# Small factors in five pieces, a second accumulator for the last attention outputs, and a reordered POOL tail in a one-core adaLN block

## The chip, the cores and the metric

The kernel runs on one NeuronCore of one Trainium2 chip. The metric is device time in microseconds of one execution. The kernel before has a median of 2770.61 us over 3 runs (2769.95 to 2776.88). In this text PE is the matrix engine, DVE the vector engine, ACT the scalar engine, POOL the GpSimd engine and SP the engine that issues the DMAs.

## The reference

One transformer block with a conditioning vector: attention over the last 512 cached keys, then a gated MLP. Everything is float32.

```python
mod = (silu(c) @ w_mod).reshape(1, 6, 1, 576)      # sa, ca, ga, sb, cb, gb
h = layernorm(x) * (1 + ca) + sa                    # x: 2048 x 576
q = h @ wq                                          # 32 heads of 128
p = softmax(q @ k[:, -512:].T * 128 ** -0.5)        # 16 key/value heads, each shared by 2 heads
x = x + ga * ((p @ v[:, -512:]) @ wo)               # wo: 4096 x 576
h = layernorm(x) * (1 + cb) + sb
x = x + gb * ((silu(h @ w1) * (h @ w3)) @ w2)       # w1, w3: 576 x 4608, w2: 4608 x 576
```

## The kernel before, in words

**Number format.** Each float32 operand of a matrix product is scaled by a power of two and split into a high and a low float16 half; a product is the sum of three float16 matmuls (high by high, high by low, low by high). The scales come from largest absolute values. For the MLP they stand in one small tile called `table`, and `act_factors` (L1180) works out from them the factors by which activations and outputs are scaled back: ten or eleven tiny DVE instructions on 4 to 28 columns, L1186 to L1199.

**Attention.** The 2048 rows are four blocks of 512. The work is a list of 128 slots, each one head on one block. A slot has four steps, t = 0 to 3, one per 128 rows. In step t, PE writes scores into a PSUM bank `pss` (L483); DVE takes the negative row maximum (L487, L488); ACT does the exponential into `p` (L500). Three of the four tiles are split on ACT and POOL and transposed by DMA; the fourth is transposed on PE into a bank `pt` (L523) and split by ACT and by DVE (`turn_low`, L552) into `ptw`. PE then forms the values `po` (L562); DVE scales them (L571), and ACT and POOL split the result into `o`.

**Output products.** Two slots make a pair. For each of the four row tiles of a pair, `back` (L428) multiplies both slots' `o` by the output weights: two pieces of six matmuls into one two-bank accumulator `E` (its tile is called `pe`, L433), and then DVE adds it to the residual `acc` (L590). Before, all pieces use the one accumulator `E`. The pieces of a pair are spread over the steps of later slots; those of the last two pairs lie in slot index n = 128 and n + 1, after the last scores.

**MLP.** The first dimension of the two input weights is cut in two and the products follow a seven-product scheme for 2 x 2 blocks: per group g of 128 hidden columns and per pair of row blocks there are seven products, in the order p1, p2, p6, p7, p5, p3, p4, each of seven matmuls (L847, into `py` or `px`). There are 36 groups for each of two pairs of row blocks. In between, DVE and ACT make the gated activations (L1017 to L1035), which are split again (L93, L94). The output products of the group pair before, called units below, are placed after single products: six matmuls (L932) into one of two accumulators that take turns, `pe` (`E`) and `pf`, and a DVE addition (L926). A counter `lane[0]` picks the accumulator, and `spare()` (L1118) returns the current one. `lane[1]` stays empty until the attention is over, and then `spare()` returns `E`. The second accumulator `pf` takes the two PSUM banks in which attention had its transposes `pt`; the pool of those (`turning`) is closed and the new one opened at L1605.

**Order.** Nothing is reordered by a scheduler: each engine runs its instructions in program order. Tasks hung on a step by `at`, `step_at` and `late_at` run in program order after that step's own work. `act_factors` runs twice: for column pairs 0 to 13 in slot 125 after step 1 (L1493), and for pairs 14 to 17 in MLP group 27 after product p2 (L1357). The first MLP group begins in slot 127, inside the attention.

**The tail.** The output products of the last group are made plainly, without the seven-product scheme: after its p6, p7, p5 and p3 there is one unit `plain(0, 0, t)` each (L934), after p4 come four units `plain(0, 1, t)`, and behind the last product four `plain(1, 1, t)` and four `plain(1, 0, t)`. Each is six matmuls into `pe` or `pf` and a DVE addition (L943). `finish` (L886) and `finish_first` (L893) add kept sums to `acc` on POOL; `finish_first(1, t)` is issued before behind `plain(0, 0, t)`. The split of the last activation, called p2 here, is made on ACT and POOL after the last product (L93, L94, tile `akv`); the p4 activation before it is split on ACT and DVE (tile `aal`).

Of the kernel before, what the change touches and what calls it, by code (L numbers as in the profile page):

```python
# [9 lines left out]
F32 = mybir.dt.float32  # L10
# [17 lines left out]
ST = SB // P  # L28
# [4 lines left out]
NF = F // P  # L33
HALF = D // 2
# [4 lines left out]
G = NF // 2  # L39
# [9 lines left out]
def tile_block(  # L49
# [14 lines left out]
    nc = tc.nc  # L64
# [16 lines left out]
    E = psum.tile([P, 2, 512], F32, tag="E", name="pe", bufs=1)  # L81
    turning = ExitStack()
# [342 lines left out]
                for k in (0, 1):  # L425
                    nc.tensor.matmul(ps, w[:, k, DC, :], hT[:, 2 * DC, :], start=False, stop=False)

    def back(o, w, t, first, last):  # L428

        rows = slice(t * P, (t + 1) * P)  # L430
        for n, (x, y) in enumerate(((0, 0), (0, 1), (1, 0))):
            for h in range(2):
                nc.tensor.matmul(  # L433
                    E[:, h, :HALF],
                    o[:, x, rows],
                    w[:, y, h * HALF : (h + 1) * HALF],
                    start=first and n == 0,
                    stop=last and n == 2,
                )
# [11 lines left out]
    n = len(slots)  # L451
# [97 lines left out]
    def turn_low(i, t):  # L549
        cols = slice(t * P, (t + 1) * P)  # L550
        pt = state[i]["pt"]
        nc.vector.tensor_sub(pt[:, 1, :, cols], state[i]["t"], pt[:, 0, :, cols])  # L552
# [30 lines left out]

    def attend_out(pair, t, j, total):
        u, _, b = slots[2 * pair]
        back(state[2 * pair + j]["o"], wos[u][:, j], t, j == 0, j == 1)
        if j == 1:
            run(*total)
            a = half_split(acc[b][:, t, :])
            nc.vector.scalar_tensor_tensor(  # L590
                a, E[:, :, :HALF], factors[:, uses[u][0], 2:3], a, op0=ALU.mult, op1=ALU.add
            )


# [131 lines left out]
    FEW = 8  # L726
# [163 lines left out]
    def finish_first(pair, t, eng):  # L890

        a = half_split(acc[2 * pair][:, t, :])
        eng.tensor_add(a, a, msums[pair][0][t])  # L893
# [40 lines left out]
    def plain(j, i, t):  # L934

        d = 2 * G - 1
        lane[0] += 1
        ps = lane[1][lane[0] % 2]
        w = osets[d, 3 if j else 4]
        multiply(ps, [(halves[d, ("p1", "p7", "p2", "p4")[2 * j + i]], w[:, h], t) for h in range(2)])  # L940
        a = half_split(acc[2 + i][:, t, :])
        factor = out_down[:, chunks(d) : chunks(d) + 1]
        nc.vector.scalar_tensor_tensor(a, ps[:, :, :HALF], factor, a, op0=ALU.mult, op1=ALU.add)  # L943
        if j == 0 and i == 0:
            finish_first(1, t, nc.gpsimd)
        elif j:
            store_out(2 + i, t)

    def act_steps(g, k):
# [98 lines left out]
    def at(i, t, task, *args):  # L1048

        tasks.setdefault((i, t), []).append((task, args))  # L1050
# [126 lines left out]
        a = works["o", p][:, 2 * part : 2 * part + 2]  # L1177
        nc.scalar.activation(a, a, AF.Copy, scale=works["n", p])

    def act_factors(lo, hi):  # L1180

        top, h_down = mlp_small[:, 2:3], mlp_small[:, 5:6]
        both = stats.rearrange("p (g j) k -> p g j k", j=2)[:, lo:hi]
        downs, pairs = both[:, :, :, 0], both[:, :, :, 1]
        a = acts_down[:, lo:hi]
        nc.vector.tensor_max(a, pairs[:, :, 0], pairs[:, :, 1])  # L1186
        nc.vector.tensor_scalar(a, a, top, 2.5 * D * 2.0**-13.5, op0=ALU.mult, op1=ALU.mult)
        nc.vector.tensor_scalar(a, a, top, 2.0**-60, op0=ALU.mult, op1=ALU.max)
        d = in_down[:, 2 * lo : 2 * hi]
        nc.vector.tensor_scalar(d, d, h_down, None, op0=ALU.mult)  # L1190
        for j in range(2):
            nc.vector.reciprocal(pairs[:, :, j], a)
            nc.vector.tensor_mul(pairs[:, :, j], pairs[:, :, j], downs[:, :, j])
        if hi == G:
            hi += 1
            nc.vector.tensor_copy(acts_down[:, G : G + 1], acts_down[:, G - 1 : G])
        d = out_down[:, lo:hi]
        nc.vector.tensor_scalar(d, d, mlp_gate_down, None, op0=ALU.mult)
        nc.vector.tensor_mul(d, d, acts_down[:, lo:hi])  # L1199

    def find(into, u, k, *key):
        find_peak(uses[u][0], k, into[(u, *key) if key else u])
# [131 lines left out]
    def late_at(step, task, *args):  # L1334
        at(("m", step // len(ORDER)), step % len(ORDER), task, *args)

    turns = len(items[ITEMS:]) // 4
    for late in range(turns):
# [15 lines left out]
            plan += [(step, make, number + k, maker, w, k), (step + STORE, store_now, number + k)]  # L1354
        for step, task, *args in plan:
            late_at(total + step, task, *args)
    late_at(2 * len(ORDER) * turns + len(ORDER) + 1, act_factors, (NF - FEW) // 2, G)  # L1357
    for k, (i, t) in enumerate(((n - 4, 0), (n - 4, 2), (n - 3, 0), (n - 2, 0))):
        at(i, t, load_wset, 0, k)

# [129 lines left out]
    at(109, 2, make_cols, "gain", "b", 4, 1.0, "T")  # L1490
    at(109, 3, lambda: spread_peaks("b", mlp_small))
    at(110, 1, lambda: scale_cols("b", t_bank(), mlp_small, 2.0**-8))
    at(n - 3, 1, act_factors, 0, (NF - FEW) // 2)  # L1493
    for b in (2, 3):
        for t in range(ST):
            at(b + 1, t, load_x, b, (t,))
# [61 lines left out]
    for i in range(n + 2):  # L1558
        run(i, -1)
        for t in range(ST):  # L1560
# [10 lines left out]
                normalize(i - 2)  # L1571
            if 1 <= i <= n and t == 2:
                turn_low(i - 1, ST - 1)
            if t == 3 and i + 1 < n:
                query_low(i + 1)
            if i < n:
# [37 lines left out]

def packed(inputs):
# [63 lines left out]
```

## Time and profile before

The profiled execution took 2773.59 us, with a span of 2771.7 us from first to last instruction.

| | |
|---|---|
| runs: median (lowest, highest) | 2770.61 us (2769.95, 2776.88) |
| profiled execution, its span | 2773.59 us, 2771.7 us |
| mean granted clock of PE | 0.992 |
| PE busy | 2692.8 us, 97% of the span |
| DVE, ACT, POOL busy | 72%, 58%, 68% |
| attention with its outputs | up to about 1632 us |
| MLP alone | from there to the end |

Every time below is in microseconds from the start of the span. A row of the timeline is start, duration, engine, line, operation, tiles (written <- read), shape and count; in square brackets stands how long the engine had been idle before it and what ended that wait. Matmuls are pipelined, so a row of six matmuls shows 0.90 us where the next may start 0.74 us after it. A row of the view by windows is the stretch, its length, the busy time and count of PE, its weight loads, DVE, ACT and POOL, then the granted PE clock, the share of the DMA engines and GB/s.

### The profile page before, as it was taken

What the parts mean: (1) busy time and instruction counts of PE and PEld (TensorE: products, weight loads), DVE (VectorE), ACT (ScalarE), POOL (GpSimd) and SP (SyncE); (2) the same over time, 40 slices, a digit from 0 to 9 for tenths busy, and PEclk for the clock granted to TensorE, in tenths of its full rate; (3) what the DMA queues carried; (4) which work ended last, traced back from release to release, by engine and by line L of the source; (5) the groups of instructions that cost most, each with busy time, mean ns of one, the idle gap of its engine ahead of it and who ended that gap; (6) DMA issues with size and microseconds to landing.
All of it is one profiled execution on the core that took longest, in us unless ns stands there. A gap on an engine that the chain in (4) does not pass through costs nothing.

```text
span 2771.7 us, 44752 instructions
## 1 busy us (share of the span) xinstructions
PE 2692.8 (97%) x15406; PEld 1515.9 (55%) x15406; DVE 1999.8 (72%) x3555; ACT 1617.5 (58%) x3013; POOL 1881.9 (68%) x1748
## 2 busy tenths in 40 slices
PE   6899999999999999999999999999999999999998
PEld 3455555555555555555555555555555555555554
DVE  7877787877788787877876667777776666666666
ACT  5777778777777778787677634544443333333332
POOL 5578788888788877777669537688873465333435
PEclk8999999999999999999999999999999999999999
DMA  5778888788787788979889935656643434333332
GB/s 184 174 174 195 196 177 192 169 184 192 160 185 167 191 186 201 206 182 213 184 190 223 239 112 171 200 170 199 213 135 108 160 121 128 104 103 111 104 110 78
DMA packets 593460, 463.84 MB, mean 167 GB/s; under 512 B 442704, under 2 KB 472528, under 8 KB 592208
## 3 DMA queue, kind: packets, MB, share of 16 engines
q1 hardware_dynamic: 592944, 460.69, 64.9%
q8 instruction: 121, 1.98, 0.3%
q14 instruction: 107, 0.88, 0.1%
q10 hardware_dynamic: 288, 0.30, 0.0%
HBM read 264.19 MB, written 95.99 MB: 130 GB/s over the span
## 4 chain that ended last, share of the span: by engine, by line
PE 52%; DVE 2%; issue 1%; ACT 1%; POOL 1%; DMA 0%; SPq 0%; DVEq 0%; ACTq 0%; POOLq 0%
PE py L847 15%; PE px L847 11%; PE pe L932 7%; PE pf L932 7%; PE pe L433 3%; PE po L562 3%; PE pss L483 3%; PE pq L410 2%; PE pt L523 0%; PE pq L414 0%; DVE table L487 0%; DVE acc L590 0%; DVE on L571 0%; DMA r<-row 0%; ACT p L500 0%
## 5 line engine op out<-in xcount | busy, mean ns | idle before, releaser
L537 POOL TENSOR_TENSOR hp<-p,hp 128x512 f16<-128x512 f32 x384 | 450.2, 1175 | 271.0 <-ACT hp L532 147.9
L500 ACT ACTIVATE p<-pss,table,factors 128x512 f32<-128x512 f32 x512 | 396.9, 775 | 360.9 <-DVE table L488 186.6
L847 PEld LDWEIGHTS <-wset 128*128 128x128 f16 x3528 | 344.6, 98 | 337.9 <-issue 5.3
L487 DVE TENSOR_REDUCE table<-pss 128x1 f32<-128x512 f32 x512 | 350.3, 684 | 209.9 <-PE pss L483 205.9
L847 PE MATMUL py<-hset,wset 128*128 128x512 f16 x2016 | 483.6, 380 | 0.0
L433 PE MATMUL pe<-o 128*128 128x288 f16 x3072 | 459.6, 286 | 15.8 <-DVE acc L590 15.3
L483 PE MATMUL pss<-k,qT 128*128 128x512 f16 x1536 | 420.1, 381 | 13.7 <-ACT p L500 10.3
L433 PEld LDWEIGHTS <-o 128*128 128x128 f16 x3072 | 300.7, 98 | 189.6 <-issue 22.4
L562 PE MATMUL po<-ptw,v 128*128 128x512 f16 x1536 | 359.3, 382 | 10.4 <-DVE ptw L552 5.5
L847 PE MATMUL px<-hset,wset 128*128 128x512 f16 x1512 | 361.6, 379 | 1.6 <-ACT p L500 1.6
L410 PE MATMUL pq<-hT,wq 128*128 128x512 f16 x1092 | 283.2, 382 | 1.0 <-POOL hT L254 0.7
L94 POOL TENSOR_TENSOR akv<-u,akv 128x512 f16<-128x512 f32 x141 | 165.0, 1180 | 174.3 <-ACT akv L93 166.5
L532 ACT CAST hp<-p 128x512 f16<-128x512 f32 x384 | 237.3, 618 | 13.2 <-POOL hT L256 0.6
L562 PEld LDWEIGHTS <-v 128*128 128x128 f16 x1536 | 148.2, 98 | 175.4 <-issue 19.4
L932 PEld LDWEIGHTS <-akv 128*128 128x128 f16 x1728 | 169.6, 98 | 93.8 <-issue 4.8
L483 PEld LDWEIGHTS <-qT 128*128 128x128 f16 x1536 | 147.9, 98 | 129.0 <-issue 15.6
L590 DVE SCALAR_TENSOR_TENSOR acc<-pe,factors,acc 128x576 f32<-128x576 f32 x256 | 207.7, 811 | 10.4 <-PE pe L433 10.4
L582 POOL TENSOR_TENSOR o<-on,o 128x512 f16<-128x512 f32 x128 | 150.4, 1175 | 55.6 <-ACT o L581 52.7
L410 PEld LDWEIGHTS <-wq 128*128 128x128 f16 x1092 | 107.5, 98 | 129.7 <-issue 4.6
L926 DVE SCALAR_TENSOR_TENSOR acc<-pf,table,acc 128x576 f32<-128x576 f32 x140 | 113.4, 810 | 80.3 <-PE pf L932 80.3
L1027 ACT COPY u<-py 128x512 f32<-128x512 f32 x72 | 42.2, 586 | 202.1 <-PE py L847 200.2
L1020 ACT ACTIVATE s<-s,table 128x512 f32<-128x512 f32 x72 | 52.0, 722 | 173.9 <-DVE s L1019 173.9
(244 smaller groups left out, 4791.2 us busy)
## 6 DMA issues: line engine op xcount, KB each, us to landing
wset<-wd SPq DMA_DIRECT2D x213, 320.0 KB, 3.2
r<-row SPq DMA_DIRECT2D x128, 256.0 KB, 3.9
oset<-od SPq DMA_DIRECT2D x106, 288.0 KB, 3.2
wraw<-in_w SPq DMA_DIRECT2D x36, 768.0 KB, 5.7
wd<-wmade SPq DMA_DIRECT2D x75, 320.0 KB, 3.3
wset<-wd SPq DMA_DIRECT2D x71, 160.0 KB, 2.3
w2raw<-in_w SPq DMA_DIRECT2D x19, 576.0 KB, 5.3
wd<-ring SPq DMA_DIRECT2D x33, 320.0 KB, 2.8
```

The costliest lines, as they stand in the source:

```text
L94: eng.tensor_sub(halves[:, 1], src, halves[:, 0])
L410: nc.tensor.matmul(ps, w[:, k // 2, m, :], hT[:, DC + m if k == 1 else m, :], start=s == 0, stop=False)
L433: nc.tensor.matmul(E[:, h, :HALF], o[:, x, rows], w[:, y, h * HALF : (h + 1) * HALF], start=first and n == 0, stop=last and n == 2,)
L483: nc.tensor.matmul(pss, q[:, x, rows], k[:, y, :], start=n == 0, stop=n == 2)
L487: nc.vector.tensor_reduce(nm[:, 0:1], pss, axis=AX.X, op=ALU.max, negate=True)
L500: nc.scalar.activation(p, pss, AF.Exp, bias=nm[:, 1:2], scale=factor, accum_out=st["l"][:, t : t + 1])
L532: nc.scalar.copy(hp[:, 0, :], state[i]["p", t])
L537: nc.gpsimd.tensor_sub(hp[:, 1, :], state[i].pop(("p", t)), hp[:, 0, :])
L562: nc.tensor.matmul(po, v[:, x, c, :], pt[:, y, c, :], start=c == 0 and n == 0, stop=c == KC - 1 and n == 2)
L590: nc.vector.scalar_tensor_tensor(a, E[:, :, :HALF], factors[:, uses[u][0], 2:3], a, op0=ALU.mult, op1=ALU.add)
L847: nc.tensor.matmul(ps, w[:, a, :], h[:, b, :], start=start and n == 0, stop=stop and n == 6, skip_group_check=True)
L932: nc.tensor.matmul(ps[:, h, :HALF], a[:, rows], w[:, b, :], start=m == 0, stop=m == 2)
```

## The change

There are three edits.

First, `act_factors` takes a piece number from 0 to 4 and issues only that part of its instructions. Each of its two calls becomes five calls in five successive steps: the early one in slot 124 after steps 2 and 3 and slot 125 after steps 0, 1 and 2, the late one in group 27 after p2, p6, p7, p5 and p3.

Second, `back` is handed its accumulator. `attend_out` advances `lane[0]` at the first piece of a row tile and asks `spare()`, and the pool of transposes is closed, and `pf` opened, in slot index 128 step 2 behind the last `turn_low`. The last two pairs' eight row tiles so use `pf` and `pe` in turn; all earlier tiles still use `pe`.

Third, `finish_first(1, t)` is issued behind `plain(1, 1, t)` instead of behind `plain(0, 0, t)`.

```diff
-    def back(o, w, t, first, last):
+    def back(ps, o, w, t, first, last):
...
-                    E[:, h, :HALF],
+                    ps[:, h, :HALF],
...
     def attend_out(pair, t, j, total):
         u, _, b = slots[2 * pair]
-        back(state[2 * pair + j]["o"], wos[u][:, j], t, j == 0, j == 1)
+        lane[0] += j == 0
+        ps = spare()
+        back(ps, state[2 * pair + j]["o"], wos[u][:, j], t, j == 0, j == 1)
...
-                a, E[:, :, :HALF], factors[:, uses[u][0], 2:3], a, op0=ALU.mult, op1=ALU.add
+                a, ps[:, :, :HALF], factors[:, uses[u][0], 2:3], a, op0=ALU.mult, op1=ALU.add
...
-        if j == 0 and i == 0:
-            finish_first(1, t, nc.gpsimd)
-        elif j:
+        if j:
             store_out(2 + i, t)
...
-    def act_factors(lo, hi):
+    def act_factors(lo, hi, piece):
...
-        nc.vector.tensor_max(a, pairs[:, :, 0], pairs[:, :, 1])
-        nc.vector.tensor_scalar(a, a, top, 2.5 * D * 2.0**-13.5, op0=ALU.mult, op1=ALU.mult)
-        nc.vector.tensor_scalar(a, a, top, 2.0**-60, op0=ALU.mult, op1=ALU.max)
-        d = in_down[:, 2 * lo : 2 * hi]
-        nc.vector.tensor_scalar(d, d, h_down, None, op0=ALU.mult)
-        for j in range(2):
+        if piece == 0:
+            nc.vector.tensor_max(a, pairs[:, :, 0], pairs[:, :, 1])
+            nc.vector.tensor_scalar(a, a, top, 2.5 * D * 2.0**-13.5, op0=ALU.mult, op1=ALU.mult)
+        elif piece == 1:
+            nc.vector.tensor_scalar(a, a, top, 2.0**-60, op0=ALU.mult, op1=ALU.max)
+            d = in_down[:, 2 * lo : 2 * hi]
+            nc.vector.tensor_scalar(d, d, h_down, None, op0=ALU.mult)
+        elif piece < 4:
+            j = piece - 2
             nc.vector.reciprocal(pairs[:, :, j], a)
             nc.vector.tensor_mul(pairs[:, :, j], pairs[:, :, j], downs[:, :, j])
...
-    late_at(2 * len(ORDER) * turns + len(ORDER) + 1, act_factors, (NF - FEW) // 2, G)
+    for piece in range(5):
+        late_at(2 * len(ORDER) * turns + len(ORDER) + 1 + piece, act_factors, (NF - FEW) // 2, G, piece)
...
-    at(n - 3, 1, act_factors, 0, (NF - FEW) // 2)
+    for piece in range(5):
+        step_at(ST * (n - 4) + 2 + piece, act_factors, 0, (NF - FEW) // 2, piece)
...
                 turn_low(i - 1, ST - 1)
+                if i == n:
+                    turning.close()
+                    after = ctx.enter_context(tc.tile_pool(name="after", bufs=1, space=PSUM))
+                    lane[1] = (E, after.tile([P, 2, 512], F32, tag="T2", name="pf"))
...
-    turning.close()
-    after = ctx.enter_context(tc.tile_pool(name="after", bufs=1, space=PSUM))
-    lane[1] = (E, after.tile([P, 2, 512], F32, tag="T2", name="pf"))
     for _ in stream:
         pass
     for i in (1, 0):
         for t in range(ST):
             plain(1, i, t)
+            if i:
+                finish_first(1, t, nc.gpsimd)
```

What remains in the last piece (4) is the copy of one column and the two instructions on `out_down`.

How rows move on DVE in MLP group 27, before. `table` holds the factors, `acc_89`, `acc_90`, `acc_91` and `acc_92` are the residual of row blocks 0 to 3, `sums` are kept sums, and L926 is the addition behind each unit:

```order
L1186 TENSOR_TENSOR table<-table 128x4
L1187 TENSOR_SCALAR table<-table 128x4
L1188 TENSOR_SCALAR table<-table 128x4
L1190 TENSOR_SCALAR table<-table 128x8
L1192 RECIPROCAL table<-table 128x4
L1193 TENSOR_TENSOR table<-table 128x4
L1192 RECIPROCAL table<-table 128x4
L1193 TENSOR_TENSOR table<-table 128x4
L1196 COPY table<-table 128x1
L1198 TENSOR_SCALAR table<-table 128x5
L1199 TENSOR_TENSOR table<-table 128x5
L926 SCALAR_TENSOR_TENSOR sums_18991<-pe,table,sums_18991 128x576
```

All eleven rows stand in one block ahead of the next addition. In the changed kernel (its lines are two to three higher: L928 is the addition, L1187 the first factor), on the same engine and place, from piece 1 on and down to the last piece:

```order
L1190 TENSOR_SCALAR table<-table 128x4
L1192 TENSOR_SCALAR table<-table 128x8
L928 SCALAR_TENSOR_TENSOR acc_89<-pf,table,acc_89 128x576
L1195 RECIPROCAL table<-table 128x4
L1196 TENSOR_TENSOR table<-table 128x4
L1028 TENSOR_TENSOR u_23232<-px,u_23232 128x512
L928 SCALAR_TENSOR_TENSOR acc_89<-pe,table,acc_89 128x576
```

```order
L1032 SCALAR_TENSOR_TENSOR u_23232<-u_23232,table,s_23261 128x512
L94 TENSOR_TENSOR aal<-u_23232,aal 128x512
L1200 COPY table<-table 128x1
L1202 TENSOR_SCALAR table<-table 128x5
L1203 TENSOR_TENSOR table<-table 128x5
L1034 TENSOR_TENSOR u_23184<-px,u_23184 128x512
L1035 SCALAR_TENSOR_TENSOR u_23184<-u_23184,table,s_23133 128x512
L928 SCALAR_TENSOR_TENSOR acc_89<-pe,table,acc_89 128x576
```

The factors now stand two or three at a time between the additions, and the last three of them stand ahead of the two steps that make the p4 activation and of the addition behind p4.

On DVE at the last two pairs' output products, in the changed kernel:

```order
L592 SCALAR_TENSOR_TENSOR acc_92<-pe,factors,acc_92 128x576
L552 TENSOR_TENSOR ptw<-pt,ptw 128x4x128
L1034 TENSOR_TENSOR u_18654<-px,u_18654 128x512
L1035 SCALAR_TENSOR_TENSOR u_18654<-u_18654,table,s_18581 128x512
L592 SCALAR_TENSOR_TENSOR acc_91<-pf,factors,acc_91 128x576
L592 SCALAR_TENSOR_TENSOR acc_91<-pe,factors,acc_91 128x576
L592 SCALAR_TENSOR_TENSOR acc_91<-pf,factors,acc_91 128x576
L592 SCALAR_TENSOR_TENSOR acc_91<-pe,factors,acc_91 128x576
```

The order of this engine is the one before; only the accumulator that is read has become `pf` for every other row tile, the first of them behind L552.

On POOL at the very end of the program, before and then in the changed kernel:

```order
L886 TENSOR_TENSOR sums<-sums 128x288
L893 TENSOR_TENSOR acc_91<-acc_91,sums 128x576 x4
L94 TENSOR_TENSOR akv<-u_29481,akv 128x512
L1674 UNCONDITIONAL_BRANCH
```

```order
L888 TENSOR_TENSOR sums<-sums 128x288
L94 TENSOR_TENSOR akv<-u_29481,akv 128x512
L895 TENSOR_TENSOR acc_91<-acc_91,sums 128x576 x4
L1683 UNCONDITIONAL_BRANCH
```

The four additions of 576 columns have changed places with the split of the last activation. The order of ACT and of SP, with all its DMAs, is the same in both kernels.

More of the change, by code (lines that the diff above doesn't have):

```diff
@@ L1185, in act_factors @@
         a = acts_down[:, lo:hi]
-        nc.vector.tensor_max(a, pairs[:, :, 0], pairs[:, :, 1])
-        nc.vector.tensor_scalar(a, a, top, 2.5 * D * 2.0**-13.5, op0=ALU.mult, op1=ALU.mult)
-        nc.vector.tensor_scalar(a, a, top, 2.0**-60, op0=ALU.mult, op1=ALU.max)
-        d = in_down[:, 2 * lo : 2 * hi]
-        nc.vector.tensor_scalar(d, d, h_down, None, op0=ALU.mult)
-        for j in range(2):
+        if piece == 0:
[7 more added lines that the diff above has]
+            j = piece - 2
             nc.vector.reciprocal(pairs[:, :, j], a)
             nc.vector.tensor_mul(pairs[:, :, j], pairs[:, :, j], downs[:, :, j])
[L1194 to L1199, printed above, removed]
+        else:
+            if hi == G:
+                hi += 1
+                nc.vector.tensor_copy(acts_down[:, G : G + 1], acts_down[:, G - 1 : G])
+            d = out_down[:, lo:hi]
+            nc.vector.tensor_scalar(d, d, mlp_gate_down, None, op0=ALU.mult)
+            nc.vector.tensor_mul(d, d, acts_down[:, lo:hi])
     def find(into, u, k, *key):
```

## The prediction

> **What bounds the kernel now.** I read the windows first, to see where PE, the engine that sets the end, is not busy, and then its waits over the whole run, the longest first.
>
> ```profile
> 1544.00:1597.00 53.00, 47.52 (x266) 26.13 (x265) 33.01 (x64) 33.25 (x65) 29.20 (x26) 1.00 1.01 252
> 1597.00:1633.00 36.00, 31.11 (x189) 18.25 (x187) 15.17 (x20) 8.62 (x14) 9.61 (x8) 1.00 0.30 90
> 2030.00:2060.00 30.00, 26.32 (x136) 14.01 (x134) 23.87 (x36) 11.00 (x19) 17.85 (x16) 0.89 0.34 106
> 2060.00:2740.00 680.00, 678.40 (x3927) 383.77 (x3925) 416.68 (x543) 215.74 (x369) 302.93 (x258) 1.00 0.38 117
> 2740.00:2771.70 31.70, 23.10 (x134) 13.49 (x132) 19.79 (x23) 3.76 (x6) 16.12 (x16) 0.93 0.20 75
> ...
> PE pe L433 <- DVE acc L590: 15.3, 15, 2.4
> PE po L562 <- DVE ptw L552: 5.5, 8, 2.9
> ```
>
> PE is busy 678.4 of 680 us in the long stretch of the MLP, so whatever delays it there is paid in full. The change touches the four short stretches, in which PE idles 5.5, 4.9, 3.7 and 8.6 us and, in the last two, also loses clock (0.89 and 0.93). In each, DVE is what PE waits for. A microsecond taken from these waits is a microsecond off the end, unless another releaser is right behind.
>
> **Early factors (slots 124 and 125).** Rows of the timeline:
>
> ```profile
> 1548.61 2.75 PE L562 MATMUL po<-ptw,v 128*128 128x512 f16 x12
> ...
> 1557.52 1.22 POOL L537 TENSOR_TENSOR hp<-p,hp 128x512 f16<-128x512 f32 x1 [0.62 <-ACT hp L532]
> 1557.75 1.02 DVE L1187 TENSOR_SCALAR table<-table 128x14 f32<-128x14 f32 x1
> 1560.19 0.59 PE L562 MATMUL po<-ptw,v 128*128 128x512 f16 x2
> 1562.02 0.18 DVE L1199 TENSOR_TENSOR table<-table 128x14 f32<-128x14 f32 x1
> 1562.96 0.68 DVE L552 TENSOR_TENSOR ptw<-pt,ptw 128x512 f16<-128x512 f32 x1
> 1563.70 2.32 PE L562 MATMUL po<-ptw,v 128*128 128x512 f16 x10 [2.91 <-DVE ptw L552]
> ```
>
> The ten instructions hold DVE from 1557.5 to 1562.1, 4.6 us for 14 columns: L1187 ends with the POOL instruction beside it, at 1558.74, so it is waiting, not computing. L552 is queued behind them, and PE's third value matmul, due two spacings of 0.22 after 1560.19, starts at 1563.70: **3.07 us lost**. The clock stays at 1.00. Cut in five, the pieces last about 1.2, 2.4, 0.4, 0.4 and 0.5 to 1.8 us. By the windows row DVE is busy 33.0 of 53 us, 28.4 without the block, so 46% is free: about 1.3 us in each step (a slot of four steps lasts 11.6, from 1548.61 to 1560.19, the same place of the next slot). Piece 1 overdraws a step by 1.1 us, and behind it stand row maxima, whose exponential PE needs two steps later. I take the whole 3.0. The lower bound is 0: PE would come 3 us earlier to the MLP's first operands, which are loaded late.
>
> ```profile
> 1582.79 0.42 SPq L699 DMA_DIRECT2D hset<-hd  x1
> 1593.75 1.67 PE L847 MATMUL py<-hset,wset 128*128 128x512 f16 x7
> hset<-hd SPq DMA_DIRECT2D x6, 1280.0 KB, 7.9
> ```
>
> Issued at 1582.79 and 7.9 us in flight, that set lands near 1590.7, 3.06 us ahead of its product. If nothing of the load moved forward, the gain would just fit; the DMA engines' share of 1.01 in this stretch says the fit may fail.
>
> **Second accumulator (last two pairs).**
>
> ```profile
> 1600.65 0.68 DVE L552 TENSOR_TENSOR ptw<-pt,ptw 128x512 f16<-128x512 f32 x1
> 1600.79 1.63 PE L433 MATMUL pe<-o 128*128 128x288 f16 x12 [0.43 <-DVE acc L590]
> 1603.50 1.63 PE L433 MATMUL pe<-o 128*128 128x288 f16 x12 [1.08 <-DVE acc L590]
> ...
> PE pe L433 <- DVE acc L590: 4.9, 5, 1.6
> ```
>
> Five of the eight row tiles start late, 4.9 us in all, since each must wait until DVE has emptied the one accumulator. Four of these waits (4.9 less 0.43) vanish, and with each 0.16 us of refilling the matmul pipeline (a six-matmul row lasts 0.90, but the next step follows after 0.73 where nothing waits; rows below): 4.46 + 0.65 = 5.1. The first tile pays: it now writes `pf`, whose banks held transposes until L552 ends at 1601.33, so it starts near 1601.4 instead of 1600.79, **0.6 later**. Queued behind it are only the tiles that gain. DVE is 42% busy here (15.2 of 36), so the additions keep up. Sum **4.5 us**; bounds 2.0, if ACT's exponential-to-silu steps of the MLP group become the next wait at two of the four places, and 4.6.
>
> **Late factors (group 27).** First the undisturbed step lengths from the chain of waits, then the timeline there, then one later group of the same kind.
>
> ```profile
> 2744.32 0.73 PE pe L932 x6
> 2745.05 1.51 PE py L847 x7
> ...
> 2036.93 1.13 DVE L1187 TENSOR_SCALAR table<-table 128x4 f32<-128x4 f32 x1
> 2038.95 1.67 PE L847 MATMUL py<-hset,wset 128*128 128x512 f16 x7
> 2042.45 1.07 DVE L1199 TENSOR_TENSOR table<-table 128x5 f32<-128x5 f32 x1
> 2044.30 1.60 PE L932 MATMUL pe<-oset,akv 128*128 128x288 f16 x6 [3.68 <-DVE sums L926]
> 2047.14 3.19 PE L847 MATMUL py<-hset,wset 128*128 128x512 f16 x7
> 2050.12 1.78 PE L847 MATMUL px<-hset,wset 128*128 128x512 f16 x7
> ...
> 2083.20 0.90 PE L932 MATMUL pe<-oset,akv 128*128 128x288 f16 x6
> 2085.95 1.04 DVE L1035 SCALAR_TENSOR_TENSOR u<-u,table,s 128x512 f32<-128x512 f32 x1
> ```
>
> The block holds DVE for 6.7 us (2036.8 to 2043.5). The unit due at 2038.95 + 1.51 = 2040.46 starts at 2044.30: 3.84. From there to 2050.12 PE needs 5.82 us for two units and one product, 2 x 0.74 + 1.51 = 2.99 at full clock: 2.83 more, the half clock after the idle time. Together **6.67 us lost**. The change does not recover all of it. Spread out, the pieces cost about 1.3, 1.9, 0.9, 0.9 and 0.5 to 2.0 us, and the last stands ahead of L1034, L1035 and the addition behind p4. In the later group, without any piece, L1035 ends at 2086.99 and the addition at 2087.8, while PE wants that accumulator again two units and two products after 2083.20, at 2087.7: there is no slack. So piece 4 (0.5 to 2.0 us) and what is left of the backlog of the others (up to 0.9) is a new PE wait of 0.5 to 2.9 us; I take 2.0, near the durations of this place, where POOL is busy throughout. Gain **4.7**; upper bound 6.2, lower 1.0 if the new wait of 2.9 is followed by as much half clock as now (2.83).
>
> **Tail.**
>
> ```profile
> L893 POOL TENSOR_TENSOR acc<-acc,sums x4: 1392/1626/1856, 2749.2 to 2754.2; 128x576 f32<-128x576 f32 x4
> ...
> 2736.83 0.75 DVE L1035 SCALAR_TENSOR_TENSOR u<-u,table,s 128x512 f32<-128x512 f32 x1
> 2738.96 0.71 DVE L94 TENSOR_TENSOR akv<-u,akv 128x512 f16<-128x512 f32 x1
> 2749.78 1.38 DVE L1032 SCALAR_TENSOR_TENSOR u<-u,table,s 128x512 f32<-128x512 f32 x1 [1.02 <-ACT s L1031]
> 2751.85 1.13 DVE L94 TENSOR_TENSOR aal<-u,aal 128x512 f16<-128x512 f32 x1 [0.69 <-ACT aal L93]
> 2753.76 0.90 PE L932 MATMUL pe<-oset,aal 128*128 128x288 f16 x6 [1.81 <-DVE acc L943]
> 2754.34 1.81 DVE L1035 SCALAR_TENSOR_TENSOR u<-u,table,s 128x512 f32<-128x512 f32 x1
> 2756.93 1.60 PE L932 MATMUL pf<-oset,aal 128*128 128x288 f16 x6 [2.27 <-DVE acc L943]
> 2766.42 0.90 PE L932 MATMUL pe<-oset,akv 128*128 128x288 f16 x6
> ```
>
> While POOL runs its four additions (2749.2 to 2755.6), three DVE steps that read SBUF twice take 1.38, 1.13 and 1.81 us; elsewhere such steps take 0.75 (L1035, and L1032 of the same form) and 0.71. They are in line, so the additions behind them, and PE, are 0.63 + 0.42 + 1.06 = **2.1 us late**. After the waits of 1.81 and 2.27 the row at 2756.93 lasts 1.60 instead of 0.90: half clock again. From it to 2766.42 nine units take 9.49 us; at 0.91 each, two accumulators' turn at full clock, it is 8.2: **1.3 us** more. With the additions moved, POOL stands still there; PE's waits shrink to about 1.0 and 1.4, and I take it that the clock holds, for a gain of **3.4**; lower bound 2.1, if it falls as before. What covers the moved additions: L1035 ends 2.1 us earlier, at 2754.05; one ACT cast (0.7, the gap from L1032 to L94) and one POOL split (1.2, as L537) later, at 2755.95, POOL is free; four additions at no more than 1.86 end by 2763.4, and the last DVE addition that needs them starts near 2763.9 (2766.42 less 3.4, plus 0.90 for its matmuls). The last is hidden by 0.5 us or more, each earlier one by more; uncovered, they would cost what they lack.
>
> The Trainium skill's page "TensorE: Matmul & The Clock Gate" (What's actually happening) has PE fall to half clock after one idle activity window of about 3.4 us, windows running freely. This trace agrees only in part: the clock fell after two gaps of 1.81 and 2.27 with a busy unit between, and did not fall after 2.91 in slot 125. By a gap limit of 3.4 us no wait left by this change would cost clock, and the sum would stay as it is.
>
> **Sum.** 3.0 + 4.5 + 4.7 + 3.4 = 15.6 us of the profiled execution's 2773.6 (span 2771.7). That execution was 3.0 us longer than the median. If these 3 us lie elsewhere, the median becomes 2770.6 - 15.6 = 2755.0; if they are lost clock at just these places, 2758.0. I take the middle, **2756.5 us**, 0.5% faster.
>
> **Rivals.**
> *B: the new waits cost clock.* The late factors give only 1.0 and the tail 2.1: 3.0 + 4.5 + 1.0 + 2.1 = 10.6, less the 1.5 by which the middle above lies short of the sum: 9.1, 2761.5. For it: the missing slack behind p4, and the clock that fell after less than 2.3 us at a stretch. Against: a single wait of 2.91 left it at 1.00.
> *C: another releaser.* PE meets the late operand loads (early factors give 0) and ACT's steps (accumulator gives 2.0): 0 + 2.0 + 4.7 + 3.4 = 10.1, less 1.5: 8.6, 2762.0. For it: the DMA share of 1.01 and a fit to 0.01 us. Against: these loads are issued behind PE-paced work and should move too.
> *D: slower.* The pieces wait longer for POOL than the blocks did. If each of the 21 small instructions waits out a whole POOL instruction of p us, the late pieces take 11p, less the 6.7 they took and the 39% of five steps (3 x 2.24 + 2.98 + 1.51 = 11.2) that DVE has free by the row of 680 us, 4.4; the early ones 10p, less 4.6 and 6.7 (46% of five steps, 14.5), plus 2.8 for a fall of the clock. PE then loses 21p - 19.6 against before; the other two edits give 7.9; so it decides from p = 1.31. At the longest addition above, 1.86, PE loses 19.5 - 7.9 = 11.6: 2782. Against: by these blocks an instruction costs 0.46 and 0.61 on average, and after an addition from PSUM POOL has moved on. In the Trainium skill, "SBUF — State Buffer" (Who interferes with whom) says that whichever of DVE and GpSimd starts first keeps the shared port pair for the whole instruction; the 1.81 us row agrees.
>
> **Chances.** Forecast 0.70, B 0.16, C 0.10, D 0.04. All upper bounds together (3.1 + 4.6 + 6.2 + 3.4 = 17.3, plus 0.7 by which the fastest run lay below the median) give 2752.6; C gives 2762. The range is 2752 to 2762.5. A measurement can tell about 0.3%, 8.3 us, from no change: the border is at 2762.3. Almost all of the forecast and rather more than half of B and of C lie below it: faster 0.86, same 0.12, slower 0.02.
>
> **What would show it.** Right: no PE wait at L562 near 1560; PE's waits on the addition L592 gone at seven of eight tiles, the first late by about 1 us behind L552; in group 27 a wait of 0.5 to 2.9 us behind p2 of the next group and full clock; in the tail L1032 and L1035 at 0.75 us and a last unit 3.4 us earlier against the last product. Wrong: a new PE wait on `hset` or on ACT in slots 126 to 129, half clock in the tail, or a last addition that waits for POOL.

## The result and the profile after

The changed kernel takes 2757.88 us (median of 6 runs, 2753.36 to 2760.39), the kernel before 2774.13 us (6 runs, 2769.95 to 2776.88). The ratio is 0.9941, with a 95% interval of 0.9929 to 0.9954: 0.6% faster. The forecast was 2756.5 us in a range of 2752 to 2762.5. The profiled execution took 2758.39 us, its span is 2756.2 us, 15.5 less than the span before.

First the windows of the changed kernel, cut within 2.5 us of the same places of the program as the windows before, and then its waits of PE (engine, line, what it waited for, us in total, times, the longest).

```profile
1540.00:1593.20 53.20, 50.52 (x283) 27.74 (x282) 34.83 (x66) 35.72 (x68) 31.27 (x27) 1.00 1.06 259
1593.20:1625.40 32.20, 31.16 (x192) 18.55 (x191) 15.69 (x23) 8.04 (x13) 10.00 (x8) 1.00 0.36 112
2022.40:2046.50 24.10, 21.83 (x118) 11.90 (x116) 20.70 (x31) 9.34 (x16) 16.45 (x15) 0.93 0.48 155
2727.00:2756.20 29.20, 22.24 (x140) 13.35 (x138) 18.51 (x25) 4.35 (x8) 16.41 (x17) 1.00 0.22 82
```
```profile
PE pe L433 <- DVE acc L592: 9.6, 10, 2.4
PE po L562 <- DVE ptw L552: 3.2, 7, 0.7
```

PE's idle time in the first two stretches went from 5.5 and 4.9 us to 2.7 and 1.0. The wait on `E` went from 15 times to 10, and the long wait at the value product, 2.9, is gone. In the third stretch the clock is still not whole (0.93); in the tail it is (1.00, before 0.93).

**By place.** Whole spans don't tell what each part is worth: at the value product of slot 124, before PE has come to anything that the change moves, the changed kernel is already 1.47 us earlier, and in the executions below this product begins anywhere between 1541.94 and 1548.61 us, although next to nothing differs up to there. So each part is measured from a PE row ahead of it to one behind it. The early place, on PE's and DVE's timeline (and then the third value product in the kernel before):

```profile
1547.14 2.75 PE L562 MATMUL po<-ptw,v 128*128 128x512 f16 x12
1558.05 0.68 DVE L552 TENSOR_TENSOR ptw<-pt,ptw 128x512 f16<-128x512 f32 x1
1558.76 2.75 PE L562 MATMUL po<-ptw,v 128*128 128x512 f16 x12
1570.34 2.75 PE L562 MATMUL po<-ptw,v 128*128 128x512 f16 x12
```
```profile
1574.84 2.75 PE L562 MATMUL po<-ptw,v 128*128 128x512 f16 x12
```

All twelve matmuls of slot 125 now run without a gap. Slots 124 and 125 take 1570.34 - 1547.14 = 23.20 us. Before, the third value product began 1574.84 - 1548.61 = 26.23 us after the first. **Gain 3.03.** The output tiles of the last two pairs, between two products of the MLP, and then the two products in the kernel before:

```profile
1594.18 1.67 PE L849 MATMUL px<-hset,wset 128*128 128x512 f16 x7
1596.89 1.64 PE L433 MATMUL pf<-o 128*128 128x288 f16 x12 [1.04 <-DVE ptw L552]
1621.83 1.67 PE L849 MATMUL py<-hset,wset 128*128 128x512 f16 x7
```
```profile
1598.68 1.67 PE L847 MATMUL px<-hset,wset 128*128 128x512 f16 x7
1630.80 1.67 PE L847 MATMUL py<-hset,wset 128*128 128x512 f16 x7
```

27.65 us between the two products; before, from 1598.68 to 1630.80, 32.12. **Gain 4.47.** The first tile waits 1.04 behind L552; no other waits. The late factors, DVE and PE from product p5 of group 27 to p7 of group 28, and then that p7 in the kernel before:

```profile
2029.98 1.67 PE L849 MATMUL py<-hset,wset 128*128 128x512 f16 x7
2038.10 1.17 DVE L1202 TENSOR_SCALAR table<-table 128x5 f32<-128x5 f32 x1
2039.30 1.19 DVE L1203 TENSOR_TENSOR table<-table 128x5 f32<-128x5 f32 x1
2042.06 0.80 DVE L928 SCALAR_TENSOR_TENSOR acc<-pe,table,acc 128x576 f32<-128x576 f32 x1
2042.91 1.60 PE L934 MATMUL pe<-oset,aal 128*128 128x288 f16 x6 [2.27 <-DVE acc L928]
2047.53 1.67 PE L849 MATMUL px<-hset,wset 128*128 128x512 f16 x7
```
```profile
2059.23 1.67 PE L847 MATMUL px<-hset,wset 128*128 128x512 f16 x7
```

17.55 us; before, from 2038.95 to 2059.23, 20.28; an undisturbed group takes 13.5. **Gain 2.73**, and 4.05 us are still lost. Of these, 2.27 is the wait, 0.16 the refilling of the pipeline, and 1.6 the clock, which the windows around the wait show (the granted clock is the third number from the end):

```profile
2039.45:2042.86 3.41, 1.19 (x6) 0.44 (x5) 3.37 (x5) 0.00 (x0) 3.41 (x3) 1.00 0.11 37
2042.86:2046.28 3.42, 3.37 (x11) 1.62 (x11) 2.14 (x4) 1.56 (x3) 1.16 (x2) 0.50 0.88 264
2046.28:2049.69 3.41, 3.41 (x22) 1.99 (x21) 0.82 (x1) 2.19 (x4) 2.60 (x4) 1.00 0.51 198
```

The tail, on PE, DVE and POOL, and then the last product in the kernel before:

```profile
2737.78 1.67 PE L849 MATMUL px<-hset,wset 128*128 128x512 f16 x7
2738.03 0.75 DVE L1032 SCALAR_TENSOR_TENSOR u<-u,table,s 128x512 f32<-128x512 f32 x1 [1.02 <-ACT s L1031]
2739.47 0.69 DVE L94 TENSOR_TENSOR aal<-u,aal 128x512 f16<-128x512 f32 x1 [0.68 <-ACT aal L93]
2741.52 0.75 DVE L1035 SCALAR_TENSOR_TENSOR u<-u,table,s 128x512 f32<-128x512 f32 x1
2743.05 0.90 PE L934 MATMUL pf<-oset,aal 128*128 128x288 f16 x6 [1.22 <-DVE acc L945]
2744.12 5.50 POOL L895 TENSOR_TENSOR acc<-acc,sums 128x576 f32<-128x576 f32 x4
2751.15 0.90 PE L934 MATMUL pe<-oset,akv 128*128 128x288 f16 x6
```
```profile
2749.54 1.67 PE L847 MATMUL px<-hset,wset 128*128 128x512 f16 x7
```

From the last product to the last unit it is 13.37 us, before 2766.42 - 2749.54 = 16.88. **Gain 3.51.** The three DVE steps are at 0.75, 0.69 and 0.75 (1.38, 1.13 and 1.81 before), the row behind the second wait lasts 0.90 instead of 1.60, and POOL's four additions end at 2749.62, ahead of the last DVE addition at 2752.15.

Together: 1.47 ahead of the change, 3.03 + 4.47 + 2.73 + 3.51 = 13.74 at the four places, and 0.29 elsewhere make the 15.5 of the spans.

### The profile page after: what moved, and what is told of

Read it like the earlier page. It is cut to its first block, busy times and chain, and to the rows that moved or that the text cites. A ratio compares the mean times of both kernels' runs of the same rounds, so it can differ in the third digit from the quotient of the medians.

```text
span 2756.2 us, 44751 instructions
## 1 busy us (share of the span) xinstructions
PE 2685.1 (97%) x15406; PEld 1512.8 (55%) x15406; DVE 1997.3 (72%) x3555; ACT 1617.8 (59%) x3013; POOL 1881.1 (68%) x1748
## 3 DMA queue, kind: packets, MB, share of 16 engines
q8 instruction: 121, 1.98, 0.3%
## 5 line engine op out<-in xcount | busy, mean ns | idle before, releaser
L433 PE MATMUL pe<-o 128*128 128x288 f16 x3024 | 453.1, 286 | 10.1 <-DVE acc L592 9.6
L483 PEld LDWEIGHTS <-qT 128*128 128x128 f16 x1536 | 147.8, 98 | 129.2 <-issue 15.5
L928 DVE SCALAR_TENSOR_TENSOR acc<-pf,table,acc 128x576 f32<-128x576 f32 x140 | 113.5, 811 | 80.8 <-PE pf L934 80.8
```

Of the source, the lines that this page charges most:

```text
L433: nc.tensor.matmul(ps[:, h, :HALF], o[:, x, rows], w[:, y, h * HALF : (h + 1) * HALF], start=first and n == 0, stop=last and n == 2,)
L483: nc.tensor.matmul(pss, q[:, x, rows], k[:, y, :], start=n == 0, stop=n == 2)
```

## The experiments

The theory at the start: the four places act each for itself, with the gains above; what is lost at the late place is the last piece alone, and the clock that falls behind its wait. The rivals: the parts help or harm each other; the wait at the late place comes from all the pieces; the tail's gain is the new order, or a POOL that is free, rather than that POOL no longer reads SBUF there.

### One part at a time

In the first three, `act_factors` has its pieces, and a call that is not spread out issues all five in one step.

The early factors alone:

```diff
...
-    at(n - 3, 1, act_factors, 0, (NF - FEW) // 2)
+    for piece in range(5):
+        step_at(ST * (n - 4) + 2 + piece, act_factors, 0, (NF - FEW) // 2, piece)
```

> Only the early factors are cut in five; the late ones stay one block, the last output products keep one accumulator, the tail is as before. Measured from the first value product of slot 124 to that of slot 126 (26.23 us before, 23.20 in the full change). Theory, each gain is made at its own place by the DVE block that is gone: 23.2, no wait of PE on the split of the transposes there, and the other three places as before (waits of 4.9, 3.7 and 1.8 + 2.3 us). Rival, the gain needs the other edits or was an accident of one execution: above 25. Rival C of the prediction, late operands: the 3 us come back as a wait on the first operand sets in slots 127 and 128.

Measured: 2768.13 us in one run (the kernel before on the same chip: 2768.4, one run). PE's value products and a later wait, and ACT ahead of that wait:

```profile
1545.31 2.75 PE L562 MATMUL po<-ptw,v 128*128 128x512 f16 x12
...
1568.51 2.75 PE L562 MATMUL po<-ptw,v 128*128 128x512 f16 x12
...
1583.00 2.28 PE L847 MATMUL px<-hset,wset 128*128 128x512 f16 x7 [1.98 <-ACT p L500]
```
```profile
1577.63 0.62 ACT L532 CAST hp<-p 128x512 f16<-128x512 f32 x1 [0.45 <-DMA ptw<-hp]
```

The two slots take 23.20 us, as in the full change, and PE waits for no operand load behind them: the 3.03 are the early pieces' own. But they were not kept in this execution. The wait of a product of the first MLP group for ACT, 1.56 in the kernel before, was 1.98, and behind it the clock was at half from 1583.92 to 1587.34: slot 126 took 18.0 us instead of 16.3, its value product 0.4 us more than before, and 2.1 of the 3.0 were gone again. In the full change a wait of 1.56 at this product left the clock at 1.00. The longer wait comes from ACT, whose cast into `hp` had first to wait 0.45 for a DMA that transposes `hp`. In the four executions with the early block, PE's wait here is 1.56 each time; in the six with early pieces it is 1.56 twice and 1.70 to 2.00 four times, each of the four behind such a wait of ACT, 0.17 to 0.47 long. So the transposes, by the releaser that the traces name, can take back 0.1 to 0.4 us of this gain; why they do so in some executions only is not settled. The other places lost what they lose in the kernel before: the same five waits on `E`, 3.67 at the late factors, 16.87 in the tail.

The second accumulator alone:

```diff
...
-        back(state[2 * pair + j]["o"], wos[u][:, j], t, j == 0, j == 1)
+        lane[0] += j == 0
+        ps = spare()
+        back(ps, state[2 * pair + j]["o"], wos[u][:, j], t, j == 0, j == 1)
...
```

> Only the second accumulator for the last two pairs; both factor blocks and the tail as before. Measured from the p4 product of MLP group 0 to the p1 product of group 2 (32.12 us before, 27.65 in the full change). Theory: 27.6, PE's waits on the addition gone at four places, the first row tile 0.6 us later behind the last split of transposes. Rival, part of it came from PE arriving at another moment after the early factors: 29 or more.

Measured: 2761.05 us, one run. PE's timeline:

```profile
1592.01 1.67 PE L849 MATMUL px<-hset,wset 128*128 128x512 f16 x7
...
1594.72 1.65 PE L433 MATMUL pf<-o 128*128 128x288 f16 x12 [1.04 <-DVE ptw L552]
...
1619.65 1.68 PE L849 MATMUL py<-hset,wset 128*128 128x512 f16 x7
```

27.64 us between the two products, against 32.12 to 32.13 in the kernels with one accumulator: the gain of 4.5 is this part's own, with the same wait of 1.04 at the first tile. The late factors (19.06) and the tail (16.83) cost about what they did. The whole time is 7 us under the 2768.4 beside it, more than the part can give; at slot 124, before any changed place, this execution is already at 1541.94, where the profiled execution before is at 1548.61: the surplus is scatter and no result. That makes the time of a single run worthless for single parts, and the stretches between two PE rows are what is compared from here on.

The late factors alone:

```diff
...
-    late_at(2 * len(ORDER) * turns + len(ORDER) + 1, act_factors, (NF - FEW) // 2, G)
+    for piece in range(5):
+        late_at(2 * len(ORDER) * turns + len(ORDER) + 1 + piece, act_factors, (NF - FEW) // 2, G, piece)
...
```

> Only the late factors are cut in five. Measured from the p5 product of group 27 to the p7 product of group 28 (20.28 us before, 17.55 in the full change, of which 1.6 is lost to half clock after a wait of 2.27). Theory 1, the wait of about 2.3 us behind the last piece always costs clock: 17.5, clock below 1 behind the wait. Theory 2, whether the clock falls depends on where the wait lies in a free-running activity window: the same wait of 2.2 to 2.4, and either 17.5 or, where the clock holds, 15.9, so that executions differ by 1.6 us at this place.

Measured: 2766.01 us, one run. PE's row at the wait, and the window that holds it:

```profile
2047.99 0.90 PE L932 MATMUL pe<-oset,aal 128*128 128x288 f16 x6 [2.27 <-DVE acc L926]
```
```profile
2043.99:2047.40 3.41, 1.73 (x9) 0.72 (x8) 3.34 (x5) 0.10 (x1) 3.41 (x4) 1.00 0.00 0
2047.40:2050.81 3.41, 2.82 (x18) 1.74 (x18) 2.58 (x4) 1.52 (x4) 1.14 (x2) 1.00 0.85 248
```

The wait is 2.27 to the hundredth, and here the clock stayed at 1.00: p5 to p7 takes 15.91 us, 1.64 less than with the full change, a gain of 20.28 - 15.91 = 4.4. So the wait belongs to the pieces, and the 1.6 of clock to something that differs between two executions of the same instructions: where the wait lies in the clock's windows, as the section on the clock shows. The two runs further down that add POOL work in the tail have the same late pieces and give one of each: 17.59 us with the clock fallen, 15.91 with it whole, both behind a wait of 2.27. The block of before is no fixed price either: in the three other runs that keep it, the clock is low for one window instead of two, and p5 to p7 takes 18.72 to 19.08 us instead of 20.28. Between 18.72 and 17.59 the gain is 1.1, between 20.28 and 15.91 it is 4.4. The unchanged block in slot 125 shows the same thing the other way about: from slot 125's first value product to that of slot 126 it is 16.34 here and 14.65 in the kernel before, since the clock fell at 1559.30 in this run and did not in that one.

The tail alone, the kernel before with

```diff
-        if j == 0 and i == 0:
-            finish_first(1, t, nc.gpsimd)
-        elif j:
+        if j:
...
             plain(1, i, t)
+            if i:
+                finish_first(1, t, nc.gpsimd)
```

> Only the four POOL additions at the end are moved behind the last split. Measured from the last p4 product to the last unit's first matmul (16.88 us before, 13.37 in the full change). Theory: 13.4, with the DVE steps that read SBUF twice at 0.7 to 0.75 us instead of 1.1 to 1.8, and full clock; if the clock falls all the same, 14.7. Rival, the tail gained because PE reached it in another phase: 15.5 or more.

Measured: 2769.51 us, one run; 14.63 from the last product to the last unit. PE's waits there are 0.75 and 1.22, as in the full change, but the clock fell behind them:

```profile
2749.92:2753.33 3.41, 1.44 (x11) 0.95 (x10) 3.37 (x6) 0.62 (x1) 0.50 (x1) 1.00 0.01 2
2753.33:2756.74 3.41, 3.41 (x16) 2.15 (x15) 1.86 (x3) 0.00 (x0) 3.41 (x4) 0.50 0.02 5
```

The gain is 2.25 instead of 3.5, the difference being one window at half clock. The shorter DVE steps are sure; the clock's share of the gain is not. So each part alone gives at its own place what it gives in the full change, except for what the clock adds or takes: the parts neither need nor harm each other.

### What the late wait is made of

The full change, with the last piece five products later, behind p7 of group 28:

```diff
-        late_at(2 * len(ORDER) * turns + len(ORDER) + 1 + piece, act_factors, (NF - FEW) // 2, G, piece)
+        step = 2 * len(ORDER) * turns + len(ORDER) + 1 + piece
+        late_at(step if piece < 4 else step + 5, act_factors, (NF - FEW) // 2, G, piece)
```

> The full change, with the last late piece (one copy and two instructions) five steps later, after p7 of group 28, where DVE has nothing queued. From p5 of group 27 to p7 of group 28: 13.47 us undisturbed, 17.55 and 15.91 with the piece where the change has it. Theory, the remaining loss comes from that piece alone, ahead of the p4 activation: no PE wait of 2.27 us, 13.5. Rival, the backlog of pieces 0 to 3 is enough: a wait of 1 us or more stays, 14.6 and up.

Measured: 2754.01 us, one run. PE at the place of the old wait, and the window over this place and the piece's new one:

```profile
2040.20 0.90 PE L934 MATMUL pe<-oset,aal 128*128 128x288 f16 x6
```
```profile
2040.00:2060.00 20.00, 20.00 (x118) 11.26 (x116) 12.91 (x20) 9.53 (x17) 15.07 (x14) 1.00 0.66 217
```

The wait is gone, PE is busy 20.00 of 20 us at full clock, and p5 to p7 takes 13.56 us, the length of an undisturbed group. So pieces 0 to 3 cost nothing, and the whole 4.05 us that the change still loses here come from the last piece. At its new place it costs PE nothing.

### What holds DVE in the tail

The full change, with four further additions on POOL at the old place of the moved ones. They add a tile, no longer needed, to itself; nothing that the outputs need is left out or changed.

```diff
-        if j:
+        if j == 0 and i == 0:
+            nc.gpsimd.tensor_add(gate_rows["a"], gate_rows["a"], gate_rows["a"])
+        elif j:
```

> The full change, with four more POOL additions of 576 columns on a tile that nobody reads any more, at the place where the four additions stood before; the moved ones stay behind the last split. Theory, DVE steps that read SBUF twice wait for POOL instructions that read SBUF: the three DVE steps at 1.1 to 1.8 us again, PE's waits 1.8 and 2.3, and 15.5 us from the last p4 product to the last unit, or 16.9 with a fall of the clock (13.4 and 14.6 in the full change).

Measured: 2761.04 us, one run. POOL's dummy additions and DVE's steps (L1034 and L1037 are L1032 and L1035 of the changed kernel):

```profile
2737.69 5.48 POOL L947 TENSOR_TENSOR gate_a<-gate_a 128x576 f32<-128x576 f32 x4
2738.26 1.12 DVE L1034 SCALAR_TENSOR_TENSOR u<-u,table,s 128x512 f32<-128x512 f32 x1 [1.02 <-ACT s L1033]
2740.07 0.87 DVE L94 TENSOR_TENSOR aal<-u,aal 128x512 f16<-128x512 f32 x1 [0.69 <-ACT aal L93]
2742.30 1.42 DVE L1037 SCALAR_TENSOR_TENSOR u<-u,table,s 128x512 f32<-128x512 f32 x1
```

The steps are longer again, by 0.37 + 0.18 + 0.67 = 1.2 us, PE's waits are 1.30 and 1.88, the clock falls, and the tail takes 15.95 us. The direction is the one expected, the size is not: the additions before cost 2.1. They took longer too, 1392 to 1856 ns each, the dummies 1146 to 1474. Why is not settled; one difference is that the dummies read the same tile twice.

The same place with fills instead, which write SBUF and read nothing:

```diff
-        if j:
+        if j == 0 and i == 0:
+            for _ in range(3):
+                nc.gpsimd.memset(gate_rows["a"], 0.0)
+        elif j:
```

> As the run with four more additions, but with twelve POOL fills of the same dead tile, which only write, for about as long. Theory, only POOL instructions that read SBUF hold DVE up: the three DVE steps at 0.7 to 0.75 us, 13.4, or 14.6 with a fall of the clock. Rival, any busy POOL there delays the end, through its order or through writes: as with the additions, 15.5 or more.

Measured: 2759.22 us, one run.

```profile
2737.46 7.58 POOL L948 MEMSET gate_a<- 128x576 f32 x12
2738.04 0.75 DVE L1035 SCALAR_TENSOR_TENSOR u<-u,table,s 128x512 f32<-128x512 f32 x1 [1.02 <-ACT s L1034]
2741.53 0.75 DVE L1038 SCALAR_TENSOR_TENSOR u<-u,table,s 128x512 f32<-128x512 f32 x1
```

POOL is busy from 2737.46 to 2745.04, across all three DVE steps, and they take 0.75, 0.69 and 0.75. So neither a busy POOL nor the order of its work held DVE, but additions that read SBUF. The tail took 14.63, with PE's waits at 0.75 and 1.22 and one window at half clock, as in the run with the tail alone.

The Trainium skill, "SBUF — State Buffer" (Who interferes with whom), says the same in general: a DVE instruction with two SBUF inputs contends with a GpSimd instruction that reads SBUF, not with one that only writes it. The two runs agree with it: 1.12 and 1.42 us beside reading additions, 0.75 beside fills.

### A version with both findings

The full change with the last piece moved as above, and with the turn of the two accumulators begun at the other one, so that the first tile takes `pe` and need not wait for the transposes' banks:

```diff
-    lane = [0, ()]
+    lane = [1, ()]
```

> The full change with the last late piece after p7 of group 28, and with the turn of the two accumulators begun the other way round, so that the first of the eight row tiles writes the old accumulator and does not wait for the last split of transposes. Theory: 13.5 us in groups 27 and 28 instead of 15.9 to 17.6, and 27.1 instead of 27.65 at the row tiles; 3 to 4.6 us less than the full change, about 2754 us where the kernel before has 2774, ratio 0.9928. Rival, the turn makes a later tile wait instead: no difference at the row tiles.

Measured: 2754.38 us (median of 5 runs, 2751.55 to 2756.36), the kernel before on that chip 2772.16 us (9 runs, 2768.78 to 2777.03); ratio 0.9931, interval 0.9917 to 0.9944. PE at the first tile, and the clock in the tail:

```profile
1597.00 1.63 PE L433 MATMUL pe<-o 128*128 128x288 f16 x12 [0.44 <-DVE acc L592]
```
```profile
2736.31:2739.72 3.41, 1.48 (x11) 1.06 (x11) 3.37 (x5) 0.62 (x1) 0.64 (x1) 1.00 0.01 2
2739.72:2743.14 3.42, 3.42 (x17) 2.16 (x16) 1.75 (x4) 0.00 (x0) 3.42 (x4) 0.50 0.03 5
```

The first tile waits 0.44 instead of 1.04, the tiles take 27.03 instead of 27.65, and p5 to p7 takes 13.56. In this execution the tail lost a window of clock (14.63). It beats the kernel before clearly. Against the change itself the medians differ by 3.5 us, but the intervals of the two ratios overlap, so that it is better by 4.0 and 0.6 us is shown at the two places only, and not in the whole time.

## Why the prediction was right

The time was right, 1.4 us from the median, three of the four terms of the sum came out to 0.1 us, and one was mis-sized. That the total fits as well as it does is partly luck: the four places gave 13.7 us in the profiled execution and not 15.6, while 16.25 us lie between the medians, and the kernel before has a median of 2774.13 in six runs, 3.5 above the 2770.61 of three from which the forecast was taken off. The runs without a profile don't show which of their places kept the clock.

**Early factors: right.** 3.0 forecast, 3.03 measured. The ten instructions in five pieces still take 5.5 us of DVE, more than the 4.6 in one block, but in five gaps. In all six executions with early pieces the two slots take 23.15 to 23.31 us, in the four with the block 26.23 or, where the clock fell, 27.92. Rival C's late operands did not appear, although PE came to them 3 us earlier: the load moved with the work that issues it, from 1582.79 to 1577.89, and its product from 1593.75 to 1589.25. What did appear, in four of the six, is a wait for ACT that is 0.1 to 0.4 us longer; a new wait for ACT there was among the prediction's signs of being wrong. The reading that DVE is what PE waits for in this stretch was not complete: 1.56 of the 5.5 us idle was this wait for ACT already before.

**Second accumulator: right.** 4.5 forecast, 4.47 measured, with the one new wait where it was put (0.6 later than before, behind L552) and of the size given (about 1; 1.04). ACT did not become the next releaser.

**Late factors: the mechanism right, the term mis-sized.** The step said: a new wait, "I take 2.0", with the clock holding after it, gain 4.7. The wait is there, behind the last piece, and 2.27 long; with 0.16 of refilling it costs 2.4 of the 6.8 us lost before. The step that failed is the other half, that the clock would hold. It fell for one window, 1.6 us, and the gain was 2.7: this is rival B at this one place, within the bounds given (1.0 to 6.2). The run with late pieces alone had the same wait and held the clock, gain 4.4. So 4.4 or 2.7 are both outcomes of this code. The 6.67 that the term set out from was one execution's too: the three other runs with the block lose 5.3 to 5.6 there. A single number for the term was false precision. What the step overlooked is a cheaper cure: with the last piece moved behind p7 the place loses nothing.

**Tail: right, and in part by chance.** 3.4 forecast, 3.51 measured: the DVE steps' 2.1 as worked out, and the clock's share. But the clock fell behind the same waits of 0.75 and 1.22 in three of the five kernels in which the tail has them (the tail alone, the fills, the last version: 14.63 us each) and held in two (the full change and the one with the moved piece: 13.37 and 13.36). The lower bound, 2.1, was nearer to what those three gave, 2.25. The tail before is 16.82 to 16.88 us in three executions and 17.69 in the run with the late factors alone, where the clock stayed low for two windows. The moved additions were hidden as forecast: they end 2.5 us ahead of the last DVE addition, where at least 0.5 had been given, since they take 1.4 us each (5.50 for four) and not the 1.86 of the longest before.

**Rival D** needed each of the 21 small instructions to wait out 1.31 us of POOL. They take 11.3 us together, 0.54 each (5.5 for the ten early ones, 5.8 for the eleven late ones). The longest, 1.17 to 1.19, come near, but only five of the 21 last over 1 us.

**The sentence on the gap limit led the wrong way.** The prediction noted that by a limit of 3.4 us on a gap no wait left would cost clock. In the changed kernel a single gap of 2.27 did, and in three others gaps of 0.75 and 1.22 did.

## What the runs showed of the clock

At the four changed places, what decides whether a wait costs clock is how busy PE is in one window of a fixed grid, not how long the wait is. In each execution the changes of the granted clock between 1.00 and 0.50 lie whole multiples of 3.413 us apart: before, the falls at 2043.50 and 2756.88 are 209.0 of them apart; with the early factors alone, the falls at 1583.92, 2041.30 and 2751.28 are 134.0 and 342.0 behind the first. Cutting the four changed stretches of all ten executions along these grids, up to PE's last unit:

| busy share of PE in a window at full clock | windows | the next window |
|---|---|---|
| 0.12 to 0.42 | 16 | half clock, all |
| 0.43 | 2 | one at half clock, one at full |
| 0.45 and more | all others | full clock, all |

So the limit lies near 0.43 of a window, about 1.5 us of work in 3.41. The rest of the ten traces from 100 us on agrees: no window up to 0.42 left the clock whole, and none from 0.45 up brought it down. In the first 90 us, where PE does other work, it does not hold: seven windows of 0.48 to 0.53 were followed by half clock and others of the same share were not. What decides there, these runs don't show. At half clock PE is nearly always busy in the next window and rises again; windows of 0.77 (before, from 2043.50) and 0.59 (late factors alone, in the tail) were followed by a second one at half clock. The limit accounts for each surprise above. The late wait of 2.27 lay in one window with a share of 1.19 / 3.41 = 0.35 in the full change, and it fell; in the run with late pieces alone the grid cut it so that the share was 1.73 / 3.41 = 0.51, and it held. The waits of 0.75 and 1.22 in the tail leave 1.44 / 3.41 = 0.42 where one window holds both (the tail alone), and 0.43 (the last version), and fall; in the full change the grid line at 2742.59 cuts the second wait, the windows on its two sides have 0.56 and 0.80, and it held. The wait of 2.91 in slot 125 fell in two executions and held in two. The start of the grid differs from execution to execution, and the runs show nothing in the kernel that sets it.

The Trainium skill, "TensorE: Matmul & The Clock Gate" (What's actually happening), has such free-running windows of 3413 ns, and the grid agrees with it. It puts the fall after an idle window; here the windows ahead of a fall were 12 to 43% busy.

## What to carry to other kernels

Tiny instructions of an in-order engine are cheap in gaps and dear in a block, and the last of them should be placed by what it stands ahead of: three instructions ahead of an addition without slack cost 2.4 to 4.0 us, and the same three five products later nothing. Where an engine's two-input steps take half as long again or more, look for another engine that reads SBUF beside them, and move that work rather than the steps. A wait of PE is to be priced with and without a window at half clock (1.3 to 1.7 us here), and such a change is to be compared place by place, since single executions differ by several microseconds ahead of the first changed place.
